# Where the two loads of x stand in the DMA queues of a decode step

## The chip, the core and the metric

The kernel runs on one NeuronCore of a Trainium2 chip. The metric is the device time of one execution in microseconds (us). Three runs of the kernel before gave 111.66, 111.83 and 113.94 us; their median is 111.83.

## What is computed

One decode step for two sequences (B = 2, one token each, width D = 448). The token x is normalised, then goes two ways: through attention over the last 2048 positions of a cache (16 query heads of 256, 8 key and value heads), and through a small ReLU network whose output, after SiLU, is multiplied onto the attention's output. All data are bf16.

```python
xn = layernorm(x)                                   # x: [2, 1, 448]
q  = (xn @ wq).reshape(2, 1, 16, 256)               # wq: [448, 4096]
k, v = last 2048 positions of k_cache, v_cache      # [2, 8, 8192, 256], each head used by two query heads
p  = softmax(q @ k^T * 256 ** -0.5)
s  = (p @ v).reshape(2, 1, 4096) @ wo               # wo: [4096, 448]
g  = silu(relu(xn @ w1) @ w2)                       # w1: [448, 1792], w2: [1792, 448]
out = x + s * g
```

## The kernel before, in words

The instructions of the five engines are written down one list per engine (`_Prog`, line 23), and each engine works through its own list in order. A dependency named by an operation becomes a wait on a semaphore ahead of it. A DMA is an entry of the list of the engine that issues it, and so it also waits in that engine's order. SyncE (SP) issues nearly all loads: this is the stream. ScalarE (ACT) issues the two loads of x and the store of the result.

The cache is worked in four units of four key heads each (u = 0 to 3); a unit is 4 MB of K and 4 MB of V. K goes to two buffers in turn (`kbuf`), V to `vbuf` (units 0, 1 and 3) or `kbuf[0]` (unit 2).

The order of the stream on SyncE is written out by hand: wq in two pieces (3 and 4 of 7 slots, lines 202 to 204), K of units 0 and 1 and V of unit 0, all issued at the start without a wait. Then K of unit 2, once DVE has transposed all of unit 0 (`do_T`, line 308); K of unit 3 after the transposes of unit 1; V of unit 1 after PV(0); V of unit 2 after the transposes of unit 2; w1 and w2 after the scores of unit 2; V of unit 3 after PV(1); and wo in five pieces.

The front, up to the first work on K, is this:

- x is loaded twice: as two rows into `x_sb` (line 194), and in the layout of the output into `x_c` (line 196; 8 partitions of 112 values, into a tile that POOL has set to zero). The second is read only by the last addition (line 535).
- ScalarE sets three PSUM banks to zero (line 221).
- DVE forms mean and variance of `x_sb` (lines 224 to 226), ScalarE takes the square root (line 228), DVE its reciprocal (line 229), and writes the normalised x spread out over `xg` (line 231).
- DVE then makes masks and selection matrices from the identity (lines 236 to 258). They don't depend on x, but stand behind `xg` in DVE's list.
- TensorE turns `xg` into columns (line 262), DVE writes them to `xr` (lines 264 to 268), and TensorE multiplies with wq: `do_q` (line 280), 28 matmuls of 512 columns, seven slots of four. The first three slots wait for the first piece of wq, the others for the second.
- q is scaled out of PSUM by DVE and ScalarE in halves (lines 295 and 298), transposed on DVE (line 301) and copied into `q_big` (line 303).

After this, for each unit: four transposes of K on DVE (`do_T`, line 311, 2.27 us each), 32 matmuls of scores (`do_S`), the row maximum (`ch_max`, lines 328 to 334), the exponential on ScalarE (line 335), a redistribution on TensorE (`ch_spread`), a masked copy on DVE (`ch_pt`, line 352) and 32 matmuls with V (`do_PV`). The units are interleaved by hand: three transposes of the next unit stand on DVE ahead of the maximum of this one, the fourth behind it. So on DVE the order is T(1) three times, max(0), T(1), pt(0), T(2) three times, max(1), T(2), and so on.

The tail has the ReLU network (`do_h` to `do_gate`), the last PV, and the product with wo: 24 of its 32 blocks in four column tiles, which are folded together, and the last eight blocks straight into the sum.

Matmuls that go through the helper `mm` have line 179 in the profile, those of q that keep the weights have line 184, and DMAs have line 37.

Of the kernel before, what the change touches and what calls it, by code (L numbers as in the profile page):

```python
# [12 lines left out]
PE, DVE, ACTE, SP, POOL = "pe", "dve", "act", "sp", "pool"  # L13
# [60 lines left out]
def bass_recurrent_scan__sliding_block_cached__dense_activation_relu__decode_kernel(  # L74
# [11 lines left out]
    B, Sq, D = A_x.shape  # L86
# [13 lines left out]
    SLOTS = 7  # L100
    HC = HD // 2
    FC = DFF // 2
    NCOL = D // 4
# [5 lines left out]
    with es:  # L109
        pr = _Prog(nc, es)  # L110

        def named(name, shape, dt):
            return es.enter_context(nc.sbuf_tensor(name, shape, dt))
# [4 lines left out]
        def view(t, off, dims, n=128, p0=0, pstep=1):  # L118
            width = t.shape[1]
            return bass.AP(t, p0 * width + off, [[width * pstep, n]] + dims)  # L120
# [11 lines left out]
        x_sb = named("x_sb", [128, D], BF)  # L132
# [11 lines left out]
        x_c = named("x_c", [128, NCOL], BF)  # L144
# [19 lines left out]
        wq_sb = kt[1]  # L164
# [24 lines left out]
        def unit_src(u, cache):  # L189
# [1 line left out]
            return cache[b, HU * hf:HU * hf + HU, SK - W:SK, :].rearrange("h (kb t) d -> kb h (t d)", t=TS)  # L191


        d_x = pr.dma(ACTE, x_sb[0:B, :], A_x[:, 0, :])
        p_xc = pr.op(POOL, lambda e: e.memset(x_c[:, :], 0.0))
        d_xc = pr.dma(ACTE, view(x_c, 0, [[1, NCOL]], n=8, pstep=16),
                      A_x[:, 0, :].rearrange("b (i n) -> i b n", i=4), [p_xc])
        wq_src = A_wq.rearrange("r (hf c) -> (r hf) c", hf=2).rearrange("(p s) c -> p (s c)", s=SLOTS)
        w1_src = B_w1.rearrange("r (hf c) -> (r hf) c", hf=2).rearrange("(p s) c -> p (s c)", s=SLOTS)
        w2_src = B_w2.rearrange("(hf p j) n -> p hf (j n)", hf=2, j=7)  # L200
        wo_src = A_wo.rearrange("(p j) n -> p (j n)", j=32)
        WQ_CUT = 3
        d_wq = [pr.dma(SP, wq_sb[:, a * HC:b * HC], wq_src[:, a * HC:b * HC])
                for a, b in ((0, WQ_CUT), (WQ_CUT, SLOTS))]
        vhome = [vbuf, vbuf, kbuf[0], vbuf]
        d_k, d_v = {}, {}

# [18 lines left out]
        v_ve = pr.op(DVE, lambda e: e.tensor_scalar(  # L226
            out=sd[0:B, 0:1], in0=st2[0:B, 1:2], scalar1=EPS, scalar2=None, op0=ALU.add), [v_ag])
        a_sd = pr.op(ACTE, lambda e: e.activation(sd[0:B, 1:2], sd[0:B, 0:1], ACT.Sqrt), [v_ve])  # L228
        v_rs = pr.op(DVE, lambda e: e.reciprocal(rstd[0:B, :], sd[0:B, 1:2]), [a_sd])
        for e2 in range(2):  # L230
            v_xn = pr.op(DVE, lambda e, e2=e2: e.tensor_scalar(  # L231
# [337 lines left out]
```

## Time and profile before

| | |
|---|---|
| median of three runs (lowest, highest) | 111.83 us (111.66, 113.94) |
| time of the profiled execution | 111.34 us |
| span of its profile | 109.7 us |
| mean granted TensorE clock | 0.827 |
| PE busy | 66.0 us, 60% of the span |
| DVE busy | 60.0 us, 55% |
| ACT busy | 12.3 us, 11% |
| POOL busy | 4.4 us, 4% |
| read from HBM | 44.11 MB, 402 GB/s over the span |
| loads of x | two, 1.8 KB each, on ScalarE's queue (28 packets with the store of the result) |
| chain that ended last | DMA 35%, DVE 32%, PE 20%, ACT 5%, SyncE's queue 3% |

The span is the time from the first to the last recorded instruction; the execution's own time is 1.64 us longer. In the timeline a line has the start, the length, the engine, the line of the code, the operation, and what it writes and reads; in brackets stands how long the engine had been idle before it, and what ended that. The chain follows the work back from the last instruction, at each step to what released it. A busy row gives the busy share of 40 equal slices in tenths. For a DMA, the time to landing counts from its issue, so it holds the time that it stands in the queue behind earlier loads.

### The profile page before, as it was taken

How to read it: one execution, taken by the hardware profiler on the slowest of the kernel's cores; microseconds unless marked ns; L12 is line 12 of the kernel's file. 1: busy time of each engine (PE TensorE's matmuls, PEld its weight loads, DVE VectorE, ACT ScalarE, POOL GpSimd, SP SyncE). 2: the span in 40 equal slices, each digit the busy share in tenths (PEclk: the TensorE clock that was granted, in tenths of full speed). 3: DMA queues.
4: the chain of work that ended last, by engine and by line, in shares of the span. 5: the costliest groups of instructions: out<-in, count | busy, mean ns of one | idle time of the engine just before them, and what ended most of it. 6: DMA issues, size and time to landing. Idle time of an engine off the chain costs nothing.

```text
span 109.7 us, 1131 instructions
## 1 busy us (share of the span) xinstructions
PE 66.0 (60%) x490; PEld 23.8 (22%) x469; DVE 60.0 (55%) x84; ACT 12.3 (11%) x21; POOL 4.4 (4%) x14
## 2 busy tenths in 40 slices
PE   0011996000009964799960899739997777857471
PEld 0000110000002204531100812044125722423130
DVE  0267003999999969201999699993004040434421
ACT  2930003500000002001001100020002202000200
POOL 7800000000000000000000000000000000000000
PEclk9999999755555699656995569997699966999999
DMA  4999999999999999999999999999899999899940
GB/s 77 408 443 442 484 430 406 430 490 406 394 466 454 406 406 466 442 406 412 466 442 394 442 481 406 406 430 478 355 418 407 424 492 430 382 397 410 398 175 1
DMA packets 2608, 44.17 MB, mean 403 GB/s; under 512 B 298, under 2 KB 556, under 8 KB 940
## 3 DMA queue, kind: packets, MB, share of 16 engines
q1 hardware_dynamic: 2576, 44.11, 94.6%
q8 instruction: 3, 0.05, 0.2%
q10 hardware_dynamic: 28, 0.01, 0.0%
q14 instruction: 1, 0.01, 0.0%
HBM read 44.11 MB, written 0.00 MB: 402 GB/s over the span
## 4 chain that ended last, share of the span: by engine, by line
DMA 35%; DVE 32%; PE 20%; ACT 5%; SPq 3%; issue 1%; POOL 1%; ACTq 0%; POOLq 0%
DVE kt L311 20%; DMA kbuf<-in_A_wo_dram 18%; DMA kbuf<-in_A_k_cache_dram 17%; PE sp L179 14%; PE sp L184 5%; SPq L37 3%; DVE q_t L301 2%; DVE q_big L303 2%; ACT e_sb L335 1%; ACT L228 1%; ACT L221 1%; DVE xg L231 1%; DVE q_n L295 1%; DVE mx L328 1%; ACT mbk L221 1%
## 5 line engine op out<-in xcount | busy, mean ns | idle before, releaser
L311 DVE STREAM_TRANSPOSE kt<-kbuf 128x2048 f32<-128x2048 f32 x16 | 35.6, 2274 | 6.4 <-DMA kbuf<-in_A_k_cache_dram 6.4
L179 PE MATMUL sp<-kt,q_big 128*8 128x512 bf16 x128 | 30.2, 1090 | 14.4 <-DVE kt L311 14.4
L179 PE MATMUL sp<-e_sb,sel 128*128 128x64 bf16 x64 | 8.1, 294 | 10.1 <-ACT e_sb L335 10.1
L179 PEld LDWEIGHTS sp<-kt,q_big 128*8 128x8 bf16 x128 | 4.9, 103 | 34.0 <-issue 18.3
L179 PEld LDWEIGHTS sp<-e_sb,sel 128*128 128x128 bf16 x64 | 6.9, 117 | 14.4 <-ACT e_sb L335 14.4
L179 PE MATMUL sp<-vbuf,pt 128*16 128x512 bf16 x96 | 7.6, 463 | 0.6 <-DVE rs L356 0.6
L335 ACT ACTIVATE e_sb<-sp,nb 128x512 bf16<-128x512 f32 x4 | 2.7, 686 | 42.7 <-DVE nb L334 42.7
L328 DVE TENSOR_REDUCE mx<-sp 128x1 f32<-128x512 f32 x4 | 2.7, 676 | 7.9 <-PE sp L179 7.9
L184 PE MATMUL sp<-kt,xr 128*128 128x512 bf16 x21 | 6.9, 446 | 0.0
L352 DVE TENSOR_TENSOR pt<-sp,hmask 128x512 bf16<-128x512 f32 x4 | 2.8, 698 | 5.2 <-PE sp L179 5.2
L295 DVE TENSOR_SCALAR q_n<-sp 128x1024 bf16<-128x1024 f32 x1 | 1.2, 1224 | 7.9 <-PE sp L184 7.9
L368 ACT ACTIVATE o_sb<-sp 128x512 bf16<-128x512 f32 x4 | 2.4, 597 | 26.4 <-PE sp L179 26.4
L179 PE MATMUL mbk<-ident,xg 2*128 2x2 bf16 x7 | 0.3, 163 | 7.9 <-DVE xg L231 7.9
L179 PEld LDWEIGHTS sp<-vbuf,pt 128*16 128x16 bf16 x96 | 4.1, 117 | 4.0 <-issue 3.5
L179 PE MATMUL sp<-kt,xr 128*128 128x512 bf16 x7 | 3.1, 445 | 2.3 <-DVE xr L268 2.3
L385 DVE TENSOR_TENSOR at_exp<-mbk,qmask 128x64 bf16<-128x64 f32 x4 | 0.8, 209 | 5.0 <-PE mbk L179 5.0
L179 PE MATMUL sp<-kbuf,pt 128*16 128x512 bf16 x32 | 3.6, 624 | 0.0
L432 DVE COPY fs<-gbk 128x448 f32<-128x448 f32 x2 | 1.2, 623 | 2.8 <-PE gbk L179 2.8
L179 PEld LDWEIGHTS sp<-kt,xr 128*128 128x128 bf16 x7 | 0.8, 114 | 8.2 <-issue 8.2
L393 DVE TENSOR_SCALAR at<-mbk,rs 64x32 bf16<-64x32 f32 x4 | 1.4, 362 | 2.0 <-PE mbk L179 2.0
L298 ACT ACTIVATE q_n<-sp 128x1024 bf16<-128x1024 f32 x1 | 1.0, 1023 | 12.0 <-PE sp L184 12.0
L301 DVE STREAM_TRANSPOSE q_t<-q_n 128x2048 bf16<-128x2048 bf16 x1 | 2.3, 2311 | 0.0
(74 smaller groups left out, 43.8 us busy)
## 6 DMA issues: line engine op xcount, KB each, us to landing
kbuf<-in_A_k_cache_dram SPq DMA_DIRECT2D x4, 4096.0 KB, 19.5
vbuf<-in_A_v_cache_dram SPq DMA_DIRECT2D x3, 4096.0 KB, 21.8
kbuf<-in_A_v_cache_dram SPq DMA_DIRECT2D x1, 4096.0 KB, 18.9
kt<-in_B_w_dram SPq DMA_DIRECT2D x2, 1568.0 KB, 15.7
kt<-in_A_wq_dram SPq DMA_DIRECT2D x1, 2048.0 KB, 10.8
kbuf<-in_A_wo_dram SPq DMA_DIRECT2D x1, 1568.0 KB, 17.1
kt<-in_A_wq_dram SPq DMA_DIRECT2D x1, 1536.0 KB, 6.4
kbuf<-in_A_wo_dram SPq DMA_DIRECT2D x1, 1120.0 KB, 19.2
```

Of the source, the lines that this page charges most:

```text
L37: o = _Op(eng, lambda e: e.dma_start(dst, src), [d for d in deps if d is not None], True)
L179: return lambda e: e.matmul(out_ap, lhsT=lhsT, rhs=rhs, start=start, stop=stop, skip_group_check=True, **kw)
L184: return lambda e: e.add_instruction(mybir.InstMatmult(name=nc.get_next_instruction_name(), start_tensor_calc=start, stop_tensor_calc=stop ...
L221: a_z = [pr.op(ACTE, lambda e, t=t: e.memzero(t[:, :])) for t in (mbk, gbk, hbk)]
L295: e.tensor_scalar(out=view(q_n, 0, [[64, 16], [32, 2], [1, 32]]), in0=view(sp, 0, [[64, 16], [1, 2], [2, 32]]), scalar1=SCALE, scalar2=Non ...
L301: v = pr.op(DVE, lambda e: e.transpose(q_t[:, :], q_n[:, :]), halves)
L303: st["q"] = pr.op(DVE, lambda e, qd=qd: e.tensor_copy(view(q_big, qd, [[NG * 32, NU], [32, NG], [4, 8]], n=32, p0=32 * qd), view(q_t, 0, [ ...
L311: st["T", u] = pr.op(DVE, lambda e: e.transpose(dst[:, 2048 * c:2048 * c + 2048], src[:, 2048 * c:2048 * c + 2048]), deps)
L328: v = pr.op(DVE, lambda e: e.tensor_reduce(out=mx[:, 0:1], in_=sbk[k], axis=AX.X, op=ALU.max), [st["S", u], p_mx, st.get("mxt")])
L335: st["exp", u] = pr.op(ACTE, lambda e: e.activation(e_sb[k][:, :], sbk[k], ACT.Exp, bias=nb[k][:, 0:1], accum_out=ssum[k][:, 0:1]), [v, st ...
L352: st["pt", u] = pr.op(DVE, lambda e: e.tensor_tensor(out=view(pt[u % 2], 0, [[128, 4], [1, 128]]), in0=view(sp, 1024, [[0, 4], [1, 128]]), ...
L368: st["osb", u] = pr.op(ACTE, lambda e: e.activation(o_sb[:, :], obk[:, :], ACT.Copy), [o, st.get(("oT", u - 1))])
```

## The change

The load of `x_sb` moves from the head of ScalarE's list to SyncE's, between the two pieces of wq. The load of `x_c` stays on ScalarE's queue, and moves in ScalarE's list from the head to the place behind the square root. The order of ScalarE's list is then: table load, three memzeros, table load, square root, the load of `x_c`, the scaling of q. SyncE's is: first piece of wq, `x_sb`, second piece of wq, K of unit 0, and on as before. The lists of DVE, TensorE and POOL keep their instructions in the same order.

```diff
--- before.py
+++ after.py
@@ -191,17 +191,16 @@
             return cache[b, HU * hf:HU * hf + HU, SK - W:SK, :].rearrange("h (kb t) d -> kb h (t d)", t=TS)
 
 
-        d_x = pr.dma(ACTE, x_sb[0:B, :], A_x[:, 0, :])
         p_xc = pr.op(POOL, lambda e: e.memset(x_c[:, :], 0.0))
-        d_xc = pr.dma(ACTE, view(x_c, 0, [[1, NCOL]], n=8, pstep=16),
-                      A_x[:, 0, :].rearrange("b (i n) -> i b n", i=4), [p_xc])
         wq_src = A_wq.rearrange("r (hf c) -> (r hf) c", hf=2).rearrange("(p s) c -> p (s c)", s=SLOTS)
         w1_src = B_w1.rearrange("r (hf c) -> (r hf) c", hf=2).rearrange("(p s) c -> p (s c)", s=SLOTS)
         w2_src = B_w2.rearrange("(hf p j) n -> p hf (j n)", hf=2, j=7)
         wo_src = A_wo.rearrange("(p j) n -> p (j n)", j=32)
         WQ_CUT = 3
         d_wq = [pr.dma(SP, wq_sb[:, a * HC:b * HC], wq_src[:, a * HC:b * HC])
-                for a, b in ((0, WQ_CUT), (WQ_CUT, SLOTS))]
+                for a, b in ((0, WQ_CUT),)]
+        d_x = pr.dma(SP, x_sb[0:B, :], A_x[:, 0, :])
+        d_wq.append(pr.dma(SP, wq_sb[:, WQ_CUT * HC:SLOTS * HC], wq_src[:, WQ_CUT * HC:SLOTS * HC]))
         vhome = [vbuf, vbuf, kbuf[0], vbuf]
         d_k, d_v = {}, {}
 
@@ -226,6 +225,8 @@
         v_ve = pr.op(DVE, lambda e: e.tensor_scalar(
             out=sd[0:B, 0:1], in0=st2[0:B, 1:2], scalar1=EPS, scalar2=None, op0=ALU.add), [v_ag])
         a_sd = pr.op(ACTE, lambda e: e.activation(sd[0:B, 1:2], sd[0:B, 0:1], ACT.Sqrt), [v_ve])
+        d_xc = pr.dma(ACTE, view(x_c, 0, [[1, NCOL]], n=8, pstep=16),
+                      A_x[:, 0, :].rearrange("b (i n) -> i b n", i=4), [p_xc])
         v_rs = pr.op(DVE, lambda e: e.reciprocal(rstd[0:B, :], sd[0:B, 1:2]), [a_sd])
         for e2 in range(2):
             v_xn = pr.op(DVE, lambda e, e2=e2: e.tensor_scalar(
```

## The prediction

> **What bounds the kernel now.** I read the page's row of DMA load first, then the chain of work that ended last, then the timeline of the first 20 us, where the change sits, and at the end the places where compute and the stream meet. From the page:
>
> ```profile
> DMA  4999999999999999999999999999899999899940
> ...
> q1 hardware_dynamic: 2576, 44.11, 94.6%
> ```
>
> After the first slice the 16 DMA engines are at nine tenths or more, with two 8s, until the last two slices. One queue, SyncE's, moves 44.11 of 44.17 MB. So the kernel is a single stream, and a change before it ends counts only where it leaves that stream without work, or where the compute behind the last bytes comes late. The chain, in order of time (start, length, what), shows where compute and stream are tied:
>
> ```profile
> 23.81 8.90 DVE kt L311 x4
> 32.71 0.02 issue
> 32.73 19.08 DMA kbuf<-in_A_k_cache_dram
> 51.80 0.02 issue
> 51.83 6.70 DVE kt L311 x3
> 58.52 0.59 DVE mx L328
> ...
> 87.78 19.25 DMA kbuf<-in_A_wo_dram
> ```
>
> The third K load is issued at 32.73, when the first K unit is transposed, and lands at 51.8. The 19.08 us are not latency: the second K unit and the first V unit are still in the queue ahead of it. So this link hides how early the issue came. From 51.83 on the chain is DVE and PE work that starts from this landing. The timeline at that place says how long DVE stood still before it, and when PE's scores of unit 1 were done:
>
> ```profile
> 51.83 6.70 DVE L311 STREAM_TRANSPOSE kt<-kbuf 128x2048 f32<-128x2048 f32 x3 [6.39 <-DMA kbuf<-in_A_k_cache_dram]
> ```
> ```profile
> 53.44 3.01 PE L179 MATMUL sp<-kt,q_big 128*8 128x512 bf16 x12
> ```
>
> DVE waits 6.39 us. The scores of unit 1 end at 53.44+3.01 = 56.45, but the row maximum over them (L328) is queued on DVE behind the three transposes, which end at 51.83+6.70 = 58.53. The front therefore has 6.39 us of room on DVE and 58.53-56.45 = 2.08 us on PE. The smaller one counts. Last, the tail:
>
> ```profile
> 107.07 0.11 PEld L179 LDWEIGHTS hbk<-kbuf,at 128*17 128x17 bf16 x8 [0.26 <-DMA kbuf<-in_A_wo_dram]
> ```
>
> Only 0.26 us of PE's time is lost to the last piece of wo. Between PV(1) at 84.35 and this point PE, ACT and DVE follow each other without a wait on a DMA, so stream and compute end almost together: compute that comes more than 0.26 us late at 58.53 moves the end.
>
> **The change, part by part.** The front as it is:
>
> ```profile
> 0.74 0.55 ACTq L37 DMA_DIRECT2D x_sb<-in_A_x_dram  x1
> ...
> 1.34 0.63 ACTq L37 DMA_DIRECT2D x_c<-in_A_x_dram  x1
> ...
> 2.48 0.62 DVE L224 BATCH_NORM_STATS2 st<-x_sb 2x6 f32<-2x448 bf16 x1 [2.48 <-DMA x_sb<-in_A_x_dram]
> ...
> 4.88 1.28 ACT L228 ACT_TABLE_LOAD   x1
> 6.18 0.20 ACT L228 ACTIVATE sd<-sd 2x1 f32<-2x1 f32 x1
> ...
> 10.56 0.59 PE L179 MATMUL sp<-kt,xr 128*128 128x512 bf16 x1 [2.30 <-DVE xr L268]
> 10.94 1.49 PE L184 MATMUL sp<-kt,xr 128*128 128x512 bf16 x3
> ```
>
> x lands at 2.48, and the variance is ready at 3.34+0.14 = 3.48. ScalarE takes it only at 6.18, since two DMA issues, a table load, three memzeros and a second table load stand before the square root there. From 6.18 to the first matmul of q at 10.56 all is serial.
>
> (a) ScalarE loses both DMA issues at its start, 0.55 and 0.63 us. Its first table load ran at 2.01 and can start near 0.75, so the second one ends near 6.17-1.25 = 4.9. Alone this would be worth 1.25 us at the front.
>
> (b) x now lands behind the first piece of wq. In the page's list of DMA issues that piece of 1536 KB lands 6.4 us after its issue at 0.73, at 7.13. Bounds: if x were not held up, it would be issued near 1.15 and take what it takes today (0.74 to 2.48, 1.74 us): 2.9. If it were held by the second piece too (10.8 us from near 1.15): 12.0. The nearest row is the load of x_c: issued at 1.34 on the other queue, all of its 12 packets move in the stretch 5.6 to 6.6, when wq's first piece ends. So I take the middle of 6.6 and 7.13, 6.9. Then DVE needs 3.51-2.48 = 1.03 to hand the variance over (three instructions of 0.62, 0.17 and 0.14, and the gaps between them), and the square root starts at 7.93 instead of 6.18. The gain of (a) is gone: ScalarE is ready at 4.9 and now waits 3 us for DVE. The front is 7.93-6.18 = 1.75 us later. Behind the wait stand all DVE instructions from L225 to L268: the masks from L236 to L258 need no x, but DVE is in order and does them after xg, so they fill nothing.
>
> (c) SyncE issues six loads instead of five before its first wait. The new one costs 0.55 by ScalarE's row, so the second piece of wq is issued by about 2.2, and K and V follow 0.55 later. The queue needs the second piece at 6 to 7 and the first K unit at 12.0 (1.15+10.8), so 4 us and more cover it: 0. The packets of x, two rows of 896 bytes in a stream of 403 GB/s: 0.
>
> (d) x_c is issued behind the square root, near 8.1, for 0.63 us on ScalarE. Its next work is q_n at 18.36, so 0. It is read at 107.71, so its landing costs 0 as well. It waited for POOL's memset of 0.73 to 0.92, which is long past. POOL's order is unchanged.
>
> (e) TensorE's clock. The first twelve matmuls of q take about 0.42 each (1.49 for three, overlapping), the last ones 0.81 for three, started every 0.86 per four. All 28 slow would be 7 x 1.66 = 11.6 us, all fast 7 x 0.86 = 6.0, against 7.77 today: -1.7 to +3.9 us. The only row is that of the same work, with a slow spell of about 3.3 us after the start; I take the same: 0.
>
> Now the sum. With 1.75 us: q starts at 12.3, the transposes of unit 0 end at 34.5 and the third K load is issued at 34.5. The queue holds work until the first V unit has landed at 3.02+38.0 = 41.0, so nothing is lost. The fourth K load goes from 43.95 to 45.7, against 51.8; the second V load from 49.16 to 50.9, against 61.3 (43.95+17.3). DVE waits 4.6 instead of 6.39 us for the landing at 51.83, which stays. Unit 1's scores end at 58.20, still before 58.53. So nothing moves after 58.53: sum 0. The profiled execution took 111.34 (span 109.7, and 1.64 around it), and the median shown is 0.49 above it, so I forecast the median again: 111.8.
>
> Where it stops being free: room of 2.08 at unit 1's scores and 0.26 at the end, 2.34 in all, of which 1.75 are used. Each us of lateness beyond 2.34 is a us of time. That is a landing of x at 2.34+5.15 = 7.5 (the delay is the landing less 5.15).
>
> [...]
>
> **The rivals.**
>
> *The slow clock in q lasts longer.* Place: the 28 matmuls of q. For it: their pace changes from 0.42 to 0.21 within this run, and their start moves by 1.75. Against it: the same 28 follow one another without a gap as before. The bounds of (e) give a delay of 0 to 5.65, so 0 to 3.3 us at the end; a third of the upper bound (+1.3: 1.75+1.3-2.34 = +0.7) gives 112.5. It decides from +0.6 us on.
>
> *x lands late, and the kernel is slower.* Place: SyncE's queue. If x's two rows come through only with the second piece of wq, at 12.0, the front is 6.85 late and the end 6.85-2.34 = +4.5, so 116.3. It counts as slower by 2% (+2.2 us) from a landing at 9.7. For it: that queue serves its loads in one row, and the second piece is issued 0.5 us behind x. Against it: x stands ahead of the second piece, and x_c's packets got through at 5.6 to 6.6.
>
> *x lands early.* If x is not held by wq's first piece, it lands at 2.9, ScalarE is ready at 4.9, and the front is up to 1.25 us earlier. The end doesn't notice: DVE waits 7.6 instead of 6.39 us for the same landing at 51.8. 111.8 again. For it: x has two rows and needs not all engines. Against it: the 6.4 us of the piece ahead.
>
> *A faster kernel* would need a stream that ends earlier; at a load of 9 in nearly every slice there is hardly a gap to close, and the change removes none. A 2% gain is 2.2 us of stream.
>
> **How the numbers follow.** All absorbed: 0.70, 111.8, own range 111.3 to 112.3 (the spread of the near runs, 111.34 to 111.83, and half a us for what is left of the room). Slow clock: 0.18, at 112.0 to 113.4 in most of its cases; above 2% in few. Late x: 0.04, 116.3. Early x: 0.06, 111.8. Something that shortens the stream: 0.02. The range reaches into the clock's cases: 111.2 to 113.3. Two per cent is about what a measurement of this kernel can tell from no change. Faster by more than that: 0.02; slower: 0.04 for the late x and 0.02 for the worst clock, 0.06; within: 0.92.
>
> **What would show it.** In the timeline of the changed kernel: ScalarE's first table load near 0.75 and its second done before 5; DVE's first instruction near 6.9, released by the DMA of x; the square root near 7.9; q's first matmul near 12.3; the third K load issued near 34.5 and landed at 51.8 as before; DVE's wait before it down from 6.39 to about 4.6; L328 of unit 1 starting at 58.5, released by nothing on PE. The DMA row stays at nines, and the last wo piece lands near 107. Wrong I would be if x landed after 7.5, if q took longer than 7.8 us by over 0.6, or if the third K load landed later than 51.8: then L328 waits for PE, and the end moves by what is over.

## The result and the profile after

The changed kernel takes 112.9 us (median of 20 executions, 112.19 to 114.59), against 112.09 us (20 executions, 111.16 to 113.94) for the kernel before: a ratio of 1.0079, with a 95% interval of 1.0056 to 1.0102. The time lies within the predicted range of 111.2 to 113.3 and within 2%, but the forecast was 111.8 and "nothing moves", and there is a small loss. Executions of one kernel spread over up to 3 us, and the ratio uses only those within 1.5% of the kernel's fastest, which leaves out more of one kernel than of another, so the difference of the means over all executions stands beside it here and below, with its 95% interval: +0.68 ± 0.48 us.

The profiled execution of the changed kernel took 112.19 us (span 110.6, mean granted clock 0.837), 0.85 more than that of the kernel before. From its page, the row of DMA load, the row of the stream's queue, and the shares of the chain by line:

```profile
DMA  3999998999999899999989999999999989999910
...
q1 hardware_dynamic: 2580, 44.11, 93.8%
...
PE sp L179 32%; DMA kbuf<-in_A_wo_dram 17%; DVE kt L312 13%; PE sp L184 5%; DMA x_sb<-in_A_x_dram 5%; ACT e_sb L336 2%; DVE q_t L302 2%; DVE mx L329 2%; DVE q_big L304 2%; SPq L37 1%; PE hbk L179 1%; DVE xg L232 1%; DVE q_n L296 1%; DVE pt L353 1%; PE gbk L179 1%
```

The stream is what it was: nines with four 8s, 44.11 MB on one queue. The chain is not. The wait for the third K load, 17% of the span before, is gone from it; PE's matmuls into `sp` (L179: the scores, the redistribution and PV) stand there with 32%, for 14% before, and the load of x with 5%.

The front, from the timeline of the changed kernel (start, length, engine, line, operation, tiles; idle time before it and what ended that):

```profile
0.73 1.28 ACT L220 ACT_TABLE_LOAD   x1 [0.73 <-PEq L555]
...
1.16 0.32 SPq L37 DMA_DIRECT2D x_sb<-in_A_x_dram  x1
...
3.61 1.28 ACT L227 ACT_TABLE_LOAD   x1
...
6.73 0.62 DVE L223 BATCH_NORM_STATS2 st<-x_sb 2x6 f32<-2x448 bf16 x1 [6.73 <-DMA x_sb<-in_A_x_dram]
...
7.76 0.20 ACT L227 ACTIVATE sd<-sd 2x1 f32<-2x1 f32 x1 [2.87 <-DVE sd L225]
7.77 1.13 ACTq L37 DMA_DIRECT2D x_c<-in_A_x_dram  x1
...
12.14 0.59 PE L179 MATMUL sp<-kt,xr 128*128 128x512 bf16 x1 [2.30 <-DVE xr L269]
...
14.22 1.49 PE L184 MATMUL sp<-kt,xr 128*128 128x512 bf16 x3
...
15.93 1.11 PE L184 MATMUL sp<-kt,xr 128*128 128x512 bf16 x3
...
17.09 0.81 PE L184 MATMUL sp<-kt,xr 128*128 128x512 bf16 x3
...
20.53 1.23 DVE L296 TENSOR_SCALAR q_n<-sp 128x1024 bf16<-128x1024 f32 x1 [8.54 <-PE sp L184]
```

x lands at 6.73 (forecast 6.9), the square root starts at 7.76 (7.93) after 2.87 us of waiting for DVE, and q starts at 12.14 (12.3). ScalarE's second table load is done at 4.89, as forecast, and gains nothing. Then comes the first surprise: the slow rows (a group of three in 1.49 us before 15.93, in 0.81 from 17.09 on) last longer, and DVE reads q at 20.53: q's matmuls took 8.36 us instead of 7.77.

Where the scores of unit 1 meet the transposes of the third K load:

```profile
50.68 6.70 DVE L312 STREAM_TRANSPOSE kt<-kbuf 128x2048 f32<-128x2048 f32 x3 [3.26 <-DMA kbuf<-in_A_k_cache_dram]
50.76 7.52 PE L179 MATMUL sp<-kt,q_big 128*8 128x512 bf16 x32
...
58.32 0.69 DVE L329 TENSOR_REDUCE mx<-sp 128x1 f32<-128x512 f32 x1 [0.94 <-PE sp L179]
```

Here is the second surprise. The K load lands at 50.68, not at 51.83, so DVE is through its three transposes at 57.38, not at 58.53. PE starts the scores of unit 1 at 50.76 and ends them at 58.28. So the row maximum (L329, which was L328) waits 0.94 us for PE, where before it waited for nothing. Still, it starts at 58.32, against 58.45 before. From the timeline of the kernel before, the maximum, the issue of the last V load, and the first instruction behind the last product with wo:

```profile
58.45 0.65 DVE L328 TENSOR_REDUCE mx<-sp 128x1 f32<-128x512 f32 x1
...
84.39 0.55 SPq L37 DMA_DIRECT2D vbuf<-in_A_v_cache_dram  x1
...
107.41 0.27 DVE L533 TENSOR_TENSOR tmp<-hbk,g_sb 128x112 f32<-128x112 f32 x1 [1.16 <-PE hbk L179]
```

In these two executions nothing is late at the maximum, the last V load is issued at 84.46 (84.39 before), and the last wo piece lands at 107.14 (107.03). The 0.85 us come behind that. The tail of the changed kernel, and then one stretch of each kernel, first after, then before (length, busy time of PE, PEld, DVE, ACT and POOL with their instructions, granted clock, DMA share, GB/s):

```profile
105.05 1.12 PE L179 MATMUL gbk<-kbuf,at 128*17 128x448 bf16 x10 [0.34 <-DMA kbuf<-in_A_wo_dram]
...
107.24 0.97 PE L179 MATMUL hbk<-kbuf,at 128*17 128x112 bf16 x32
108.25 0.27 DVE L534 TENSOR_TENSOR tmp<-hbk,g_sb 128x112 f32<-128x112 f32 x1 [1.42 <-PE hbk L179]
```
```profile
106.00:107.00 1.00, 0.28 (x6) 0.11 (x8) 0.62 (x1) 0.00 (x0) 0.00 (x0) 0.50 0.10 38
```
```profile
106.00:107.00 1.00, 0.68 (x32) 0.52 (x32) 0.25 (x1) 0.00 (x0) 0.00 (x0) 1.00 0.09 34
```

At the end of the changed kernel TensorE ran at half clock, from 105.27 on by the clock's records; the last ten of the 24 products with wo in column tiles took 1.12 us, and DVE could use the products that follow 0.84 us later than before (108.25 for 107.41). At that place the kernel before ran at full clock. So one pair of profiles puts the whole difference in the clock of the tail. Whether that is the cause or this pair's chance had to be tried.

### The profile page after: what moved, and what is told of

The parts are those of the page before. It is cut to its first block, busy times and chain, and to the rows that moved or that the text cites. A ratio compares the mean times of both kernels' runs of the same rounds, so it can differ in the third digit from the quotient of the medians.

```text
span 110.6 us, 1131 instructions
## 1 busy us (share of the span) xinstructions
PE 67.1 (61%) x490; PEld 24.8 (22%) x469; DVE 60.2 (54%) x84; ACT 12.3 (11%) x21; POOL 4.4 (4%) x14
## 3 DMA queue, kind: packets, MB, share of 16 engines
q1 hardware_dynamic: 2580, 44.11, 93.8%
HBM read 44.11 MB, written 0.00 MB: 399 GB/s over the span
## 4 chain that ended last, share of the span: by engine, by line
PE 41%; DVE 28%; DMA 22%; issue 2%; ACT 2%; SPq 1%
PE sp L179 32%; DMA kbuf<-in_A_wo_dram 17%; DVE kt L312 13%; PE sp L184 5%; DMA x_sb<-in_A_x_dram 5%; ACT e_sb L336 2%; DVE q_t L302 2%; DVE mx L329 2%; DVE q_big L304 2%; SPq L37 1%; PE hbk L179 1%; DVE xg L232 1%; DVE q_n L296 1%; DVE pt L353 1%; PE gbk L179 1%
## 5 line engine op out<-in xcount | busy, mean ns | idle before, releaser
L179 PE MATMUL sp<-kt,q_big 128*8 128x512 bf16 x128 | 29.9, 1082 | 14.4 <-DVE kt L312 14.4
L179 PE MATMUL sp<-e_sb,sel 128*128 128x64 bf16 x64 | 8.1, 294 | 8.2 <-ACT e_sb L336 8.2
L179 PEld LDWEIGHTS sp<-kt,q_big 128*8 128x8 bf16 x128 | 5.2, 101 | 33.4 <-issue 17.7
L179 PEld LDWEIGHTS sp<-e_sb,sel 128*128 128x128 bf16 x64 | 7.0, 119 | 12.5 <-ACT e_sb L336 12.5
L179 PE MATMUL sp<-vbuf,pt 128*16 128x512 bf16 x96 | 7.4, 457 | 0.6 <-DVE rs L357 0.6
L329 DVE TENSOR_REDUCE mx<-sp 128x1 f32<-128x512 f32 x4 | 2.8, 690 | 8.9 <-PE sp L179 8.9
L184 PE MATMUL sp<-kt,xr 128*128 128x512 bf16 x21 | 7.3, 468 | 0.0
L179 PE MATMUL mbk<-ident,xg 2*128 2x2 bf16 x7 | 0.3, 163 | 9.5 <-DVE xg L232 9.5
L179 PEld LDWEIGHTS sp<-vbuf,pt 128*16 128x16 bf16 x96 | 4.1, 117 | 3.9 <-issue 3.4
L179 PE MATMUL sp<-kt,xr 128*128 128x512 bf16 x7 | 3.4, 481 | 2.3 <-DVE xr L269 2.3
L223 DVE BATCH_NORM_STATS2 st<-x_sb 2x6 f32<-2x448 bf16 x1 | 0.6, 617 | 6.7 <-DMA x_sb<-in_A_x_dram 6.7
L179 PE MATMUL sp<-kbuf,pt 128*16 128x512 bf16 x32 | 3.2, 574 | 0.0
L179 PEld LDWEIGHTS sp<-kt,xr 128*128 128x128 bf16 x7 | 0.8, 114 | 8.8 <-issue 8.8
L179 PE MATMUL gbk<-kbuf,at 128*17 128x448 bf16 x24 | 2.0, 410 | 0.8 <-DVE at L394 0.5
```

The source lines that it names most:

```text
L179: return lambda e: e.matmul(out_ap, lhsT=lhsT, rhs=rhs, start=start, stop=stop, skip_group_check=True, **kw)
L184: return lambda e: e.add_instruction(mybir.InstMatmult(name=nc.get_next_instruction_name(), start_tensor_calc=start, stop_tensor_calc=stop ...
L329: v = pr.op(DVE, lambda e: e.tensor_reduce(out=mx[:, 0:1], in_=sbk[k], axis=AX.X, op=ALU.max), [st["S", u], p_mx, st.get("mxt")])
```

## The experiments

Theory 1: the later front is the cause. x behind wq's first piece makes q start 1.6 us later, the room behind it is smaller than the profile of before showed, and what is over it makes everything behind the row maximum of unit 1 late. Theory 2: the new places in the queues cost something by themselves (x_c behind the square root, x between the pieces of wq). Theory 3: neither; the clock in the tail falls differently, and the difference is chance or comes from there. In both profiles the clock's records change only after multiples of 3.41 us, from the first at 13.74 in the kernel before and from 16.52 in the changed kernel: such a step is what the expectations call a window, and its place in an execution the phase.

In each row of the table, the difference is that of the means against the kernel before, from the second row on measured on the same chip. The rows stand for 12 executions each, but 20 in the first, 6 of e6 and 11 of f5.

| kernel | median us (lowest to highest) | difference, us | ratio (95% interval) |
|---|---|---|---|
| changed kernel, first set | 112.90 (112.19–114.59) | +0.68 ± 0.48 | 1.0079 (1.0056–1.0102) |
| after_again | 113.14 (111.25–114.88) | +0.87 ± 0.69 | 1.0053 (1.0003–1.0104) |
| e1_xc_only | 112.85 (112.30–114.36) | +0.26 ± 0.43 | 1.0087 (1.0049–1.0125) |
| e1_again | 112.66 (111.88–113.91) | +0.56 ± 0.47 | 1.0072 (1.0028–1.0115) |
| e2_xsb_only | 113.39 (111.94–114.53) | +0.75 ± 0.47 | 1.0093 (1.0048–1.0137) |
| e3_delay2 | 112.72 (111.31–114.65) | +0.08 ± 0.57 | 1.0020 (0.9966–1.0075) |
| e6_delay4 | 114.57 (114.17–116.94) | +2.66 ± 0.89 | 1.0229 (1.0174–1.0284) |
| e4_after_masks_first | 112.28 (111.46–113.17) | −0.38 ± 0.43 | 1.0020 (0.9969–1.0070) |
| f1_before_warm | 111.00 (110.87–113.01) | −0.93 ± 0.46 | 0.9915 (0.9879–0.9951) |
| f1_before_warm_again | 111.62 (110.67–112.52) | −0.70 ± 0.48 | 0.9948 (0.9908–0.9988) |
| f4_xc_only_warm | 111.34 (110.75–112.30) | −0.96 ± 0.43 | 0.9947 (0.9910–0.9983) |
| f2_after_warm | 112.29 (111.21–113.65) | 0.00 ± 0.61 | 0.9992 (0.9943–1.0040) |
| f3_delay4_warm | 114.14 (112.36–116.65) | +1.76 ± 0.77 | 1.0081 (1.0029–1.0132) |
| f5_before_keep12 | 111.16 (110.82–112.66) | −1.10 ± 0.44 | 0.9936 (0.9902–0.9970) |
| f6_after_keep12 | 111.64 (110.81–113.68) | −0.55 ± 0.62 | 0.9947 (0.9913–0.9982) |
| f7_delay4_keep12 | 113.28 (111.58–115.24) | +0.85 ± 0.70 | 1.0051 (0.9996–1.0106) |
| h_early_front_keep12 | 112.21 (110.97–113.91) | −0.21 ± 0.64 | 0.9975 (0.9934–1.0016) |

### One part at a time

e1 moves only the load of x_c behind the square root and leaves `x_sb` at the head of ScalarE's list; e2 moves only `x_sb` to SyncE's list.

```diff
 e1 (against the kernel before)
-        d_xc = pr.dma(ACTE, view(x_c, 0, [[1, NCOL]], n=8, pstep=16),
-                      A_x[:, 0, :].rearrange("b (i n) -> i b n", i=4), [p_xc])
...
         a_sd = pr.op(ACTE, lambda e: e.activation(sd[0:B, 1:2], sd[0:B, 0:1], ACT.Sqrt), [v_ve])
+        d_xc = pr.dma(ACTE, view(x_c, 0, [[1, NCOL]], n=8, pstep=16),
+                      A_x[:, 0, :].rearrange("b (i n) -> i b n", i=4), [p_xc])
```
```diff
 e2 (against the kernel before)
-        d_x = pr.dma(ACTE, x_sb[0:B, :], A_x[:, 0, :])
...
-                for a, b in ((0, WQ_CUT), (WQ_CUT, SLOTS))]
+                for a, b in ((0, WQ_CUT),)]
+        d_x = pr.dma(SP, x_sb[0:B, :], A_x[:, 0, :])
+        d_wq.append(pr.dma(SP, wq_sb[:, WQ_CUT * HC:SLOTS * HC], wq_src[:, WQ_CUT * HC:SLOTS * HC]))
```

> Only the load of x_c is moved behind the square root; x_sb stays at the head of ScalarE's queue. Theory 1 (front: the late landing of x makes the front 1.6 us later, q's slow clock varies on top, and what exceeds the room at unit 1's scores moves the end): x lands near 2.5, ScalarE loses one DMA issue of 0.6, q starts near 10.0 instead of 10.56, and the time is that of the kernel before, ratio 0.997 to 1.003. Theory 2 (queue: one of the two loads in its new place makes the stream longer, the last wo piece lands later): if it is x_c's place, 1.008; otherwise 1.000. Theory 3 (tail: TensorE's clock in the last 5 us is lower by chance of the window's phase): no order between kernels, ratio within 1.000 plus or minus 0.003.

> Only the load of x_sb is moved to SyncE's queue behind the first piece of wq; x_c stays at the head of ScalarE's queue. Theory 1: x lands near 6.7, q starts near 12.1, ratio 1.008 like the whole change. Theory 2: 1.008 if it is x_sb's place in the stream, 1.000 if it is x_c's. Theory 3: within 1.000 plus or minus 0.003.

e2 alone gives what the whole change gives: +0.75 ± 0.47. x lands at 7.02 there and q starts at 12.43. e1 makes the front 0.67 us earlier (q at 9.89) and is not faster: +0.26 ± 0.43. Its ratio, 1.0087, is as high as the changed kernel's. That looked like a price of x_c's new place, so it was taken again, with the changed kernel beside it on the same chip:

> Only the load of x_c moved, once more. Its front is 0.7 us earlier than before's. Theory 1: the mean is that of the kernel before, within 0.2 us, and the 0.3 us seen the first time was chance. Theory 2: 0.3 us or more above, again.

> The changed kernel once more, beside the kernel before on another chip, since the times of one kernel spread over 3 us and the means of so few runs are uncertain by 0.2 us. Theory 1: the mean over all runs 0.3 to 0.8 us above the kernel before. Theory 3: the first difference was chance; within 0.2 us.

The changed kernel's loss came back (+0.87 ± 0.69), and so did e1's (+0.56 ± 0.47; with the first set the mean is +0.41 ± 0.32, so it is hardly chance, though the front is earlier). In e1's second profile q's matmuls take 9.1 us, so that DVE reads q at 19.00, later than the 18.36 of before, and the front's gain is gone; yet the row maximum of unit 1 starts at 58.31 without a wait, and the last V load is issued at 84.46, so no step of it is late before the tail. In the second profile of the changed kernel the maximum waits 0.73 us for PE and starts at 58.26.

### A delay without the change, and the change without the delay

e3 is the kernel before with the two writes of `xg` done once more on DVE, e6 with these writes done twice more. What is computed stays the same; the front gets 1.4 and 2.8 us later. e4 is the changed kernel with the masks of DVE (which need no x) ahead of the statistics, so that they fill the wait for x.

```diff
 e3 (e6 has "* 2")
+        for e2 in [0, 1] * 1:
+            v_xn = pr.op(DVE, lambda e, e2=e2: e.tensor_scalar(
+                out=view(xg, 128 - 127 * e2, [[256, 4], [128, 2], [2, 64]], n=B),
+                in0=view(x_sb, 3 * e2, [[1, 4], [0, 2], [SLOTS, 64]], n=B),
+                scalar1=st2[0:B, 0:1], scalar2=rstd[0:B, 0:1],
+                op0=ALU.subtract, op1=ALU.mult), [v_xn])
```

> The kernel before with both loads where they were, and the two writes of the normalised x (0.67 us each) done twice in a chain: the front is 1.4 us later with no load moved. Theory 1: q starts near 12.0, ratio 1.005 to 1.008. Theory 2: the stream is that of before, 1.000. Theory 3: within 1.000 plus or minus 0.003.

> The kernel before with the two writes of the normalised x done three times in a chain: the front is 2.8 us later, with both loads where they were. Theory 1 (front), now with its size from the profiles so far: the maximum of unit 1 starts at the later of two times, the third K load's landing plus 6.7 us (57.4 to 58.6 in six profiles) and the end of unit 1's scores (56.45 plus the delay, plus up to 1.5 us of slow clock in q). With 2.8 us the scores end at 59.2 to 60.7, so DVE waits for TensorE there, and the mean over all runs is 1.0 to 2.0 us above the kernel before. Theory 2 (queue): no change. Theory 3 (the clock's phase in the tail and nothing else): no change of the mean beyond 0.3 us.

> The changed kernel with the masks (which need no x) ahead of the statistics of x on DVE, so that they fill the wait for x. Theory 1: x lands at 6.7, but q starts 1.3 us earlier than in the changed kernel, near 10.8, within 0.3 us of the kernel before, and the time goes back to it: ratio 0.998 to 1.003. Theory 2: both loads stay in their new places, 1.008. Theory 3: within 1.000 plus or minus 0.003.

The timelines at the place where scores and transposes meet, e3, e6, e4 and e2 in this order:

```profile
50.28 7.51 PE L179 MATMUL sp<-kt,q_big 128*8 128x512 bf16 x32
...
57.85 0.69 DVE L334 TENSOR_REDUCE mx<-sp 128x1 f32<-128x512 f32 x1
```
```profile
51.55 7.52 PE L179 MATMUL sp<-kt,q_big 128*8 128x512 bf16 x32
...
59.13 0.69 DVE L334 TENSOR_REDUCE mx<-sp 128x1 f32<-128x512 f32 x1 [1.69 <-PE sp L179]
```
```profile
50.78 6.70 DVE L312 STREAM_TRANSPOSE kt<-kbuf 128x2048 f32<-128x2048 f32 x3 [5.01 <-DMA kbuf<-in_A_k_cache_dram]
...
57.40 0.65 DVE L329 TENSOR_REDUCE mx<-sp 128x1 f32<-128x512 f32 x1
```
```profile
51.11 6.70 DVE L312 STREAM_TRANSPOSE kt<-kbuf 128x2048 f32<-128x2048 f32 x3 [3.89 <-DMA kbuf<-in_A_k_cache_dram]
...
57.88 0.69 DVE L329 TENSOR_REDUCE mx<-sp 128x1 f32<-128x512 f32 x1
...
84.04 0.55 SPq L37 DMA_DIRECT2D vbuf<-in_A_v_cache_dram  x1
```

With 1.4 us the scores end at 57.79 and the maximum follows at 57.85, 0.1 us after DVE had finished its transposes: the room is used up to the last tenth, and no loss shows (+0.08 ± 0.57, which doesn't exclude 0.6). With 2.8 us DVE idles 1.69 us, the maximum starts at 59.13, and the kernel loses 2.66 ± 0.89. In e4, where both loads stand in their new places but q starts at 10.67, DVE waits for nothing and the loss is gone (−0.38 ± 0.43; e2, on the same chip, is 1.13 ± 0.50 above it). So the new places alone don't make the loss, and a front that is late enough does cost time.

That the changed kernel loses by the same wait isn't shown. e2 has as large a loss, but its maximum comes 0.07 us behind DVE's own work, at 57.88, and its last V load goes out at 84.04; both are earlier than in the kernel before (58.45 and 84.39). And e1 loses with an earlier front. The size doesn't fit either: e6's maximum is 0.68 us later than the 58.45 of before, its last V load 0.86 us (85.25), and its loss is three to four times that.

The reason that the room was smaller than the 2.08 us of the prediction is the landing of the third K load. In the kernel before, 15 of the 16 landings that the trace has for this load (read here as one for each of the 16 DMA engines) had come by 50.67, and the last came at 51.80. A fetch of instructions ran just then, from 49.80 to 50.77. The DMA queues of the kernel before in the stretch from 49.5 to 51 us have this row (packets, MB, share of 16 engines):

```profile
q8 instruction: 1, 0.02, 4.0%
```

One packet of 16 KB with 4.0% of 16 engines over 1.5 us is one engine for 0.96 us. The trace doesn't name the engine, so that it is the late one is inferred from time and size. In the changed kernel 16 KB are fetched at 52.19, after the landing, and the K load is whole at 50.68. There it is the next load, the fourth of K, that has one late landing: 15 had come by 60.34, the last came at 61.30. This repeats in all the profiles taken: wherever the fetch starts by 50.1 (kernel before, e1, f1, f4, f5, h), the landing is at 51.5 to 52.1; wherever it starts at 50.8 or later (changed kernel, e2, e3, e4, e6, f2, f3, f6, f7), the landing is at 50.7 to 51.1. In seven of the nine profiles with the early fetch the landing comes 2.0 us after the fetch's start (in f4 and h 3.1). With one exception (e4, whose landing is early at an early front) it is the kernels with a later q that fetch later. So it seems that a later front takes away part of its own cover: the transposes end 1.1 us sooner, and 2.08 us of room are about 1. What sets off the fetch isn't known.

### The clock in the tail

From the issue of the last V load to the last product the profiles without idle matmuls need 23.0 us (before) to 25.1 (e2 and e6), and what differs is the length of the stretches at half clock in it. The kernel before is the shortest of the nine: the changed kernel needs 23.8 and 24.8 in its two profiles, e1 24.0 and 24.9, e3 24.8, e4 24.6. In the six from 24.6 on, the clock is at half for 10.24 us, from between 86.0 and 88.8 on, and again from between 106.5 and 109.3 on; in the kernel before for 3.41 us, from 88.83 on. e4, which has no loss, is among the six, and e1 and the changed kernel have one profile on either side. So these stretches move a single execution by up to 2 us, in kernels with and without the loss, and no pair of profiles can show a loss of 0.7 us.

To see what this is worth, f1 is the kernel before with matmuls that nobody reads ("idle matmuls"): 128x384, into the unused part of a PSUM bank, put into TensorE's list where it waits. f4 has the same with e1's move, f2 with the whole change, f3 with e6's delay. In what was expected of them, theory A is direct lateness, as in theory 1, and theory B says that a later front only moves TensorE's work against the clock's stretches at full and at half speed (multiples of 3.41 us by the records, the windows of f2's expectation).

```diff
+        def keep(n):
+            deps = [v_sel] + [st.get(("r", u)) for u in range(NU)]
+            for _ in range(n):
+                pr.op(PE, mm(xbk[:, 128:512], ident[:, :], sel[:, 0:384], True, True), deps)
...
         do_o_pe(0)
+        keep(20)
         ch_spread(1)
...
         ch_max(2)
+        keep(11)
         ch_spread(2)
```

(Nine more such places follow, of 1 to 6 matmuls each.)

> The kernel before with matmuls that nobody reads (ident times 384 columns of sel, 0.16 us each at full clock, into unused columns of xbk) in TensorE's idle places from 56 us on: 20 before the redistribution of unit 1, 11 before that of unit 2, 6 after PV(1), 1 to 3 at each short wait of the tail. Theory 3 (the spread of the times is the clock's phase in the tail): the granted clock stays 1.0 from about 57 us to the last matmul, from the issue of the last V load to the last product takes 23 us or less (before it is 23.0 in the profile at hand, 24 to 25.2 in four profiles of other kernels with the same tail), and the time is 111.3 or less. Theory 1 (front) has no say here. If the spread has another cause, the clock changes and the time stays within 111.2 to 114.

> The kernel before with matmuls that nobody reads in TensorE's idle places from 56 us on. If the clock's phase in the tail makes the spread of the times, the mean falls by 0.4 us or more and the spread (highest less lowest) shrinks from 3 us to below 2.2. If not, both stay.

> The kernel before with matmuls that nobody reads in TensorE's idle places from 56 us on, as the base of the three beside it: mean about 0.9 us below the kernel before, as in its first timing.

> Only the load of x_c moved, with the idle matmuls. Its front is 0.7 us earlier, so theories A and B both say: within 0.2 us of the kernel before with the idle matmuls. If it is 0.3 us or more above, as it was without them in two timings (0.3 and 0.6, each uncertain by 0.45), the place of x_c's load has a price of its own in the stream.

A single execution took 111.95 us against 112.93 for the kernel before. That is above the 111.3 expected, and the clock did not stay at 1.00: it was at half from 75.42 to 78.83 and from 89.08 to 92.49. Over more of them f1 is faster by 0.93 ± 0.46 and, on another chip, by 0.70 ± 0.48. And f4, e1's move with the same idle matmuls, is as fast as f1 (−0.96 ± 0.43 against −0.70 ± 0.48 on the same chip; its own mean is 0.26 ± 0.44 below f1's). So with the idle matmuls x_c behind the square root shows no cost, which points to the clock for e1's small loss without them.

> The changed kernel with the same idle matmuls, so that the clock in the tail no longer differs. Theory A (direct lateness: unit 1's scores end later, and all behind them): the mean lies 0.4 to 0.8 us above the kernel before with the idle matmuls. Theory B (the later front only moves TensorE's work against the clock's windows, and the tail falls into slow ones more often): within 0.2 us of it.

> The kernel before with the front 2.8 us later and the idle matmuls. Theory A: the mean 1.5 to 2.6 us above the kernel before with the idle matmuls (without them it was 2.7). Theory B: at most 0.9 us above it, which is what the issue of the last V load shows (85.25 against 84.4), and the rest of the 2.7 us is the clock in the tail.

These two failed as a measure. In f2 the maximum starts at 59.01, and the 20 idle matmuls beside it run from 59.0 to 62.4, past the end of the exponential near 61.2, on which PE waits at that place: they lengthen the path themselves. So 20 became 12, in the kernel before (f5), the changed kernel (f6) and the kernel with e6's delay (f7):

> The kernel before with the idle matmuls, but 12 instead of 20 behind unit 1's scores: 20 take 3.4 us, which is longer than the 2.3 us from the scores' end to the end of the exponential, so in the kernels with a late front they were themselves in the way. Base of the three beside it; mean 0.6 to 1.0 us below the kernel before.

> The changed kernel with the same. Theory A (direct lateness of unit 1's scores): mean 0.3 to 0.7 us above the kernel before with the same idle matmuls. Theory B (only the clock in the tail): within 0.2 us of it, and the 0.7 us seen with 20 idle matmuls were those matmuls.

> The kernel before with the front 2.8 us later, with the same idle matmuls. Theory A: mean 1.0 to 1.9 us above the kernel before with them. Theory B: at most 0.5 us.

f5 is 1.10 ± 0.44 us faster than the kernel before. Three stretches of the tail, in the kernel before and in f5, by the windows of the trace (columns as above):

```profile
85.00:90.00 5.00, 3.52 (x35) 2.70 (x39) 1.24 (x4) 0.66 (x2) 0.00 (x0) 0.88 1.03 427
90.00:95.00 5.00, 3.97 (x36) 1.39 (x29) 0.59 (x2) 0.60 (x1) 0.00 (x0) 0.78 0.99 426
...
105.00:108.00 3.00, 1.55 (x50) 0.72 (x42) 1.17 (x3) 0.00 (x0) 0.00 (x0) 1.00 0.15 57
```
```profile
85.00:90.00 5.00, 3.94 (x50) 2.98 (x51) 1.24 (x4) 0.58 (x2) 0.00 (x0) 1.00 1.04 439
90.00:95.00 5.00, 4.57 (x39) 1.82 (x28) 1.24 (x4) 0.60 (x1) 0.00 (x0) 1.00 1.05 449
...
105.00:108.00 3.00, 3.00 (x53) 1.29 (x45) 0.62 (x1) 0.00 (x0) 0.00 (x0) 0.55 0.11 41
```

The clock rises from 0.88 and 0.78 to 1.00, but in the last stretch it falls from 1.00 to 0.55: the idle matmuls shorten the time at half clock and don't end it. All ten profiles with idle matmuls have such a stretch behind 88 us, of 3.4 to 6.8 us, and need 22.7 to 23.8 us from the last V load to the last product. This execution of f5 took 111.85 us, 0.5 more than the profiled one of the kernel before, so the gain of 1.10 us shows in the means and not in this pair.

With these idle matmuls a cost of the change can't be told from none: the mean of f6 is 0.55 ± 0.66 us above that of f5, and the ratios of the two to the kernel before, 0.9947 and 0.9936, are nearly the same. The difference of the means comes from f6's longest executions: 4 of its 12 lie above 112.5, against 1 of 11 of f5. The delay of 2.8 us costs 1.95 ± 0.73 us (f7 less f5). In f6 and f7 the maximum waits for PE; f7's row:

```profile
59.50 0.69 DVE L334 TENSOR_REDUCE mx<-sp 128x1 f32<-128x512 f32 x1 [2.15 <-PE sp L179]
```

That is 1.04 us later than f5's 58.46, and the last V load goes out at 85.23, 0.92 us later than f5's 84.31.

Last, a version that was to beat all: x at the head of ScalarE's list as before, x_c behind the square root, the masks ahead of the statistics, and the 12 idle matmuls. Against f5 only the front differs.

> A version that may beat both: x_sb stays at the head of ScalarE's queue, x_c behind the square root, the masks ahead of the statistics of x on DVE, and the idle matmuls. q starts near 8.6 instead of 10.56, so unit 1's scores end near 54.5 whatever the clock does. Theory A: the spread on the side of the front is gone; mean 0 to 0.3 us below the kernel before with the idle matmuls, 110.9 to 111.5. If the front had no say, the same as it within 0.1.

This missed. q starts at 8.57, the maximum at 58.15 with no wait, and the median is 112.21 us; the mean is 0.89 ± 0.67 us above f5's. A front that is 2 us earlier gives nothing, as the prediction said of the rival with the early x, but why it is worse than f5 is not settled. Like e1, it speaks against lateness alone.

### The clock in all executions

Every execution has a span and a mean clock. Over the 32 executions of the changed kernel above and 133 of the kernel before, those taken beside the experiments (for the 20 of the first set there are no spans), the spans are 111.52 and 110.76 in the mean, +0.75 ± 0.31, and the clocks 0.809 and 0.814. Fitted together, a clock lower by 0.01 goes with 0.19 us more span; the 0.005 between the kernels are worth 0.09 us of the 0.75, and 0.66 ± 0.28 us remain at the same mean clock. So the loss is hardly chance, and a lower mean clock is not what makes it (the chips are not all the same, though, so this is no strict pairing). The mean says nothing of where the slow stretches fall, though, and these executions have no timeline. They also show where the profile of the kernel before stands: only 13 of the 133 have a span of 109.7 us or less.

## Why the prediction was wrong

**Right: the mechanism at the front.** x lands with wq's first piece (6.73 for 6.9; the 16 landings of that piece come from 6.38 to 7.12, those of the second from 11.24 to 11.93), so the late-x and early-x rivals are out. The square root, the start of q (12.14 for 12.3) and the issue of the third K load (34.90 for 34.5) are where they were put, apart from q's length. ScalarE's gain of 1.25 us is lost in its wait of 2.87 us for DVE. Steps (a) and (b) stand.

**Right as far as shown: (c) and (d) at nothing.** The second piece of wq is issued at 1.54 and K at 1.94, and the stream's load is unchanged. For x_c's place e4 and f4 show no price; e1's +0.41 ± 0.32 over its two sets leaves a doubt.

**Wrong: (e), the clock of q "the same: 0".** q took 8.36 us for 7.77. In the trace of before, TensorE goes to full clock at 13.74, 3.2 us after q's start; in that of after at 16.52, 4.4 us after it. At half speed (0.43 us for 512 columns, against 0.215), 1.2 us more of slow matmuls are 0.6 us. Over all the profiles q takes 7.8 to 9.1 us, so 7.77 was the short end of a spread that the one row could not show. The slow spells of q measured 3.2 to 5.9 us over the profiles, for the 3.3 that (e) took. The clock's records of the two kernels change only after multiples of 3.41 us (3.41, 6.83, 10.24, 13.65, 17.07); what decides when the slow spell of q ends isn't shown. The prediction named the rival of a longer slow clock, gave it 0.18, and priced it at +0.7 us.

**Wrong: the room of 2.08 us.** This is the step that failed: "Unit 1's scores end at 58.20, still before 58.53. So nothing moves after 58.53: sum 0." The 58.53 was taken to stay, since the stream did not change. But the K load landed at 50.68 instead of 51.83, and the transposes ended at 57.38. The 1.1 us were not the stream's, as far as the trace shows: one landing of 16 was late, by 1.1 us, and just before it a fetch of instructions ran on another queue, for 0.96 us. That the fetch delayed it is inferred, not shown. So of the room of about 2 us one half was there only as long as the front was early, and the scores, 1.83 us later than before (58.28 for 56.45), went over it: DVE waits 0.94, 0.73 and 0.76 us for PE in three profiles with the whole change (the changed kernel twice, and f6), and for nothing in those of the kernel before, e1, f1, f5 and h. In e2, which has the late x too, it waits 0.07 us. So the step is wrong at this place; that this wait is what makes the 0.7 us isn't shown.

**Missing: the clock behind 58 us.** The sum has no term for it: (e) prices the clock for q alone, and behind 58.53 the timeline of the one profile is taken to stay. The tail from the last V load on takes 23.0 to 25.1 us over the nine profiles without idle matmuls, and the one that was read is the shortest of them. A smaller slip in reading that tail: a weight load waits 0.32 us at 104.84 for another piece of wo, so PE and its loads did not run from 84.35 to 107.07 without a wait on a DMA.

**The size.** The prediction's own rule, that the end moves by what is over the room, would give the changed kernel's profile no loss at all, since the maximum is at 58.32 against 58.45. What it could give over many executions is this: before, q's spread of about 1.3 us was swallowed by the room; now it goes through to the end. f6's executions spread more than f5's, as they should by it, but the 20 of the changed kernel in the first set spread less than those of the kernel before. It is a reading, not shown: no execution without a profile has a timeline. And of the 1.1 us between the forecast of 111.8 and the 112.9 measured, 0.26 are no part of the change: the 20 executions of the kernel before have a median of 112.09, the three that the forecast went by 111.83.

**What stays open.** What makes the 0.7 us: this lateness, or a tail whose slow stretches fall differently, or both. For the first speak e6 and f7 (2.66 and, against f5, 1.95 us at a front 2.8 us later), e4, and the +0.66 at the same mean clock; for the second the pair of profiles, where all of it lies behind 105 us, e2, which loses without a wait for PE, e1, which loses with an earlier front, and e6, whose loss is three times its lateness. f6 less f5, which was to settle it, has zero within its interval. Open also: why h is not as fast as f5.

## What to carry to other kernels

A room read from one profile is the difference of two instants, and each must be asked what holds it: here the later instant was held by one late landing of 16 (51.80, the others by 50.67), beside a fetch of instructions that moved with the change (49.80 before, 52.19 after). Where a change makes a front later by nearly the whole room, take the room less the spread of what lies in between (here 0 to 1.3 us of slow clock in q), and don't forecast that nothing moves. Where a serial tail's clock changes from execution to execution, one profile says little of its length (here 23.0 to 25.1 us), and a small loss is read from many executions. And filling TensorE's waits there is worth trying ahead of any shuffling of loads: in f1, f4 and f5 it gave 0.7 to 1.1 us, more than the change moved, though with h's early front no gain showed (−0.21 ± 0.64).

## What the runs showed of the hardware

- The 16 KB fetch of instructions took 0.96 us in the kernel before (at 49.80) and 0.97 in the changed kernel (at 52.19), each as one packet. Of the 4 MB load of K that it ran beside, the last of 16 landings came about 1 us behind the other 15 (51.80 and 50.67 in the kernel before, 61.30 and 60.34 in the changed kernel). That the fetch held up that share is inferred.
- The load of x_c moved late beside the large loads of the other queue: issued at 7.77 on the otherwise idle queue, it moved its 12 packets between 12.14 and 14.93, after the second piece of wq had landed at 11.93; before, issued at 1.34, between 5.7 and 6.5.
- The scores' 32 matmuls of a unit took the same time at either clock: 7.52 us at 50.76 in the changed kernel, at full clock, and 7.52 at 32.75 in the kernel before, two thirds of it at half clock. The 32 of PV took 3.62 us at half clock (unit 0, at 45.51 in the kernel before) and 2.05 at full (at 82.30).
- The granted clock reads 1.00 in the windows of q's slow spell, which lie ahead of the clock's first record (13.74 in the kernel before, 16.52 in the changed kernel); only the pace of the matmuls (0.43 us for 512 columns, then 0.215) shows it there.
